# Three key tiles' halves kept in the second token group's buffer, with the hand-written order of steps rearranged

## The chip, the core and the metric

The kernel runs on one core of a Trainium2 chip. The metric is the device time of one execution in microseconds (us). Five engines take part: TensorE (PE, with its weight loads as PEld), VectorE (DVE), ScalarE (ACT), GpSimd (POOL) and SyncE (SP), which here only issues DMAs. Each engine works through its own queue in order. Tensors lie in on-chip memory in tiles of 128 partitions; PSUM holds the results of products.

## The reference

Local attention of 4 batches, 8 heads, 768 tokens, head size 64, and behind it a gated feed-forward layer over 3072 tokens (512 wide, 1536 inside):

```python
k_sum = k.reshape(B, H, nb, 32, D).max(axis=3)          # 24 block summaries
v_sum = v.reshape(B, H, nb, 32, D).mean(axis=3)
scores_l = scale * q @ k.T, masked to |i - j| < 16
scores_s = scale * q @ k_sum.T + log(32)
a = softmax(concat(scores_l, scores_s))
x = a @ concat(v, v_sum)                                # heads side by side: 512 wide
xn = x / sqrt(mean(x * x) + 1e-6) * rms_g
out = (silu(xn @ w_gate) * (xn @ w_val)) @ w_out
```

## The kernel before, in words

Tokens go in 24 units of 128 (six to a batch) and the feed-forward in token groups of 384, 128, 256 and then 384 tokens (`GROUPS`). Units 0 to 2 take a warm-up path of their own (`su_...` steps, float32). From unit 3 on a unit runs `load_unit`, `prep_q`, `prep_k`, `fill_k`, `prep_v`, `scores` and `expo` (twice, four heads each), `attend`, `norm_a` and `norm_b`. A group then runs, for each of twelve blocks f of 128 inner columns, `gate_val` (24 products into two PSUM tiles, then tanh and two multiplications) and `project` (the product with the output weights, added up in PSUM).

Precision is kept by splitting: a number is scaled by a power of two and held as a half-precision part and the half-precision rest. Weights are decoded and split on the way in (`decode_gv`, `split_gv`, `decode_o`); twelve gate and value blocks n, of which a pair (n even and odd) serves two f. `pow2` (L282) makes the powers of two in the small tiles `w_t`, `w_s`, `w_i`; `w_t` has one buffer.

The steps that the change touches:

- `split_k` (L468) makes the halves of a key tile in `khl`: ScalarE casts (L470), VectorE subtracts (L471), and SP transposes the result by DMA into `kT` (L476). `khl` has one buffer of 128 x 1024 half-precision numbers. `prep_k` (L493) calls it for tiles of 128 keys, `split_ks` (L465) for the block summaries (32 rows, into `ksT`).
- `fill_k` (L538) copies beside a key tile's own columns the summaries (from `ksT`), the last columns of the tile before (VectorE) and the first of the tile behind (GpSimd). `scores` (L561) of a unit needs the fills.
- `norm_b` (L803) transposes a normalised unit into its group's `xT`. The pool `xp` has two such buffers of 6144 half-precision numbers a partition, taken in turn by the groups.
- `sum_load` (L400) loads a piece of keys or values into `hn` (two buffers) and `sum_fold` (L412) reduces it, keys on VectorE and values on GpSimd.

`PLAN` (L43) is the list of steps. It gives the order in which instructions are written down, and thereby their priority: the build places each instruction on its engine's queue by a simulation of its own, when what it needs is ready there. So an engine's order follows `PLAN` without being the same.

Of the kernel before, what the change touches and what calls it, by code (L numbers as in the profile page):

```python
# [77 lines left out]
project 1 10 128 384; swap_att 3; gate_val 2 0 256; prep_k 9; gate_val 2 1 256; norm_a 6; project 2 0 256 512;  # L78
scores 7 1; gate_val 2 2 256; sum_load 2 0 0 2; fill_k 8; project 1 11 128 384; project 2 1 256 512;
sum_fold 2 0 0 0; load_k 10; scores 8 0; sum_fold 2 0 0 1; load_unit 9; sum_fold 2 0 0 2; gate_val 2 3 256; expo 7 1;  # L80
project 2 2 256 512; expo 8 0; sum_load 2 0 0 3; prep_q 9; project 0 11 384 0; prep_k 10; sum_fold 2 0 0 3;
gate_val 2 4 256; prep_k 11; scores 8 1; sum_load 2 0 1 0; prep_v 7; sum_load 2 0 1 1; expo 8 1; gate_val 2 5 256;
# [817 lines left out]
```

## Time and profile before

| | us |
|---|---|
| median of 3 runs (788.92 to 789.74) | 789.23 |
| the profiled execution | 787.48 |
| its span, first to last instruction | 785.7 |

| engine | busy us | share of the span |
|---|---|---|
| PE | 697.0 | 89% |
| DVE | 519.9 | 66% |
| ACT | 444.8 | 57% |
| POOL | 243.0 | 31% |

The span is the time from the first to the last instruction; the rest of an execution lies around it. An idle time of an engine is put down to what ended it (the releaser). An instruction waits for its engine's earlier ones as well as for its own inputs, so a releaser can be late because it stood behind another wait.

### The profile page before, as it was taken

Reading aid. Unit: us, or ns where it says so; the run is one execution under the profiler, and the core shown is the slowest. Engines: PE = TensorE matmul, PEld = TensorE weight load, DVE = VectorE, ACT = ScalarE, POOL = GpSimd, SP = SyncE. Lnnn points to the kernel's source line nnn. Section 1 sums busy time; section 2 is a strip of 40 time slices with the busy share of each in tenths; the row PEclk is TensorE's granted clock in tenths of the full one; section 3 lists DMA queues with packets and bytes.
Section 4 is the critical chain, followed back from the end, with each engine's and each line's share of the span. In section 5 each row is a group of like instructions: output and inputs, shape, how many; then the busy total and the mean of one; then the engine's idle time right before and its main releaser. Section 6 shows DMA issues by size and latency. Waiting matters only on the chain.

```text
span 785.7 us, 13988 instructions
## 1 busy us (share of the span) xinstructions
PE 697.0 (89%) x4880; PEld 488.5 (62%) x4880; DVE 519.9 (66%) x1466; ACT 444.8 (57%) x918; POOL 243.0 (31%) x334
## 2 busy tenths in 40 slices
PE   3871796629889999999999999999999999999997
PEld 2571454427667786666666665666666666666665
DVE  5799686967687686856767676677666664543222
ACT  3699857967556575744656565656455453421111
POOL 7355101554232244432223253422232221200000
PEclk9775798859999999999999999999999999999999
DMA  9944976578857947756756856775457452201001
GB/s 230 331 151 138 257 160 171 130 159 168 162 114 147 183 110 169 165 109 123 125 122 140 149 128 159 135 145 99 110 108 120 85 122 44 38 15 41 1 1 40
DMA packets 270547, 100.21 MB, mean 128 GB/s; under 512 B 254212, under 2 KB 254308, under 8 KB 270476
## 3 DMA queue, kind: packets, MB, share of 16 engines
q1 hardware_dynamic: 260700, 80.61, 50.7%
q10 hardware_dynamic: 7968, 16.78, 6.4%
q0 software_dynamic: 1808, 1.93, 1.1%
q8 instruction: 38, 0.62, 0.4%
q14 instruction: 33, 0.27, 0.1%
HBM read 51.38 MB, written 6.64 MB: 74 GB/s over the span
## 4 chain that ended last, share of the span: by engine, by line
PE 60%; DMA 15%; DVE 9%; issue 4%; SPq 4%; ACT 4%; POOL 4%; DVEq 0%; POOLq 0%; ACTq 0%
PE gv L829 36%; PE acc L854 18%; DMA kT<-khl 4%; PE att L614 3%; DMA hn<-in_k_dram 2%; DMA hn<-in_v_dram 2%; PE att L573 2%; SPq L484 2%; DMA qT<-qs 1%; DMA kr_l<-in_k_dram 1%; DVE khl L471 1%; POOL ee L226 1%; DMA eT<-ee 1%; PE acc L688 1%; DMA v1f<-in_v_dram 1%
## 5 line engine op out<-in xcount | busy, mean ns | idle before, releaser
L829 PE MATMUL gv<-xT,w_gv 128*128 128x384 f16 (+2 forms) x2592 | 408.8, 314 | 41.5 <-DMA xT<-xs 26.9
L829 PEld LDWEIGHTS <-w_gv 128*128 128x128 f16 x2592 | 241.4, 100 | 183.7 <-issue 56.4
L854 PE MATMUL acc<-wo,hh 128*128 128x512 f32 x576 | 188.9, 415 | 5.8 <-ACT hh L221 4.4
L226 POOL TENSOR_TENSOR ee<-sm,ee 128x512 f16<-128x512 f32 x84 | 84.1, 1020 | 151.1 <-ACT ee L221 117.1
L854 PEld LDWEIGHTS acc<-wo,hh 128*128 128x128 f32 x576 | 104.6, 190 | 26.5 <-ACT hh L221 5.0
L834 DVE SCALAR_TENSOR_TENSOR th<-th,gv 128x384 f32<-128x384 f32 (+2 forms) x108 | 54.5, 505 | 94.3 <-ACT th L833 94.0
L854 PE MATMUL acc<-wo,hl 128*128 128x512 f32 x288 | 111.1, 402 | 3.1 <-DVE hl L226 2.9
L588 ACT ACTIVATE sm<-sm,mx,c 128x192 f32<-128x192 f32 x168 | 78.4, 536 | 57.7 <-DVE mx L580 57.7
L833 ACT ACTIVATE th<-gv,f_sc 128x384 f32<-128x384 f32 (+2 forms) x108 | 57.8, 535 | 72.7 <-PE gv L829 68.1
L221 ACT CAST hh<-th 128x384 fp32r<-128x384 f32 (+2 forms) x108 | 51.0, 473 | 77.5 <-DVE th L835 76.6
L226 DVE TENSOR_TENSOR hl<-th,hh 128x384 fp32r<-128x384 f32 (+2 forms) x108 | 66.9, 619 | 40.3 <-ACT hh L221 39.9
L835 DVE SCALAR_TENSOR_TENSOR th<-th,f_sc,gv 128x384 f32<-128x384 f32 (+2 forms) x108 | 61.2, 567 | 27.6 <-PE gv L829 24.1
L854 PEld LDWEIGHTS acc<-wo,hl 128*128 128x128 f32 x288 | 53.7, 189 | 17.2 <-DVE hl L226 6.0
L577 DVE CUSTOM_DVE_ANT_0 sm<-att,mask 128x192 f32<-128x192 f32 x168 | 51.0, 350 | 11.3 <-POOL ee L226 9.7
L555 POOL DMA_DIRECT2D v2h<-v2h x42 | 22.9, 545 | 95.3 <-ACT v2h L554 95.3
L573 PE MATMUL att<-kT,qT 128*128 128x192 f16 x336 | 38.7, 253 | 10.3 <-DMA qT<-qs 9.9
L419 ACT ACTIVATE junk<-hn 96x512 uint8<-96x512 f32 x48 | 30.0, 626 | 24.2 <-DMA hn<-in_v_dram 14.3
L226 POOL TENSOR_TENSOR xs<-x,xs 128x512 f16<-128x512 f32 x24 | 31.6, 1317 | 34.5 <-ACT xs L221 32.5
L573 PEld LDWEIGHTS <-qT 128*128 128x128 f16 x336 | 27.1, 100 | 21.7 <-DMA qT<-qs 12.0
L221 ACT CAST ee<-sm 128x512 f16<-128x512 f32 x84 | 38.5, 506 | 3.7 <-DMA eT<-ee 3.5
L614 PEld LDWEIGHTS <-eT 128*128 128x128 f16 x840 | 30.8, 99 | 8.8 <-issue 6.6
L425 POOL TENSOR_TENSOR hn<-hn 96x512 f32<-96x512 f32 x18 | 25.3, 1408 | 24.9 <-DMA hn<-in_v_dram 22.3
(162 smaller groups left out, 876.6 us busy)
## 6 DMA issues: line engine op xcount, KB each, us to landing
out_dram<-ob ACTq DMA_DIRECT2D x23, 256.0 KB
hn<-in_k_dram SPq DMA_DIRECT2D x24, 192.0 KB
hn<-in_v_dram SPq DMA_DIRECT2D x24, 192.0 KB
qr_l<-in_q_dram SPq DMA_DIRECT2D x17, 256.0 KB
vr_l<-in_v_dram SPq DMA_DIRECT2D x17, 256.0 KB
raw<-in_moe_w_val_dram ACTq DMA_DIRECT2D x4, 1024.0 KB
kr_l<-in_k_dram SPq DMA_DIRECT2D x16, 256.0 KB
raw<-in_moe_w_gate_dram ACTq DMA_DIRECT2D x3, 1024.0 KB
```

The lines of the kernel that those rows point to most:

```text
L221: nc.scalar.copy(o, i)
L226: (nc.vector if ENG.get(op, "p") == "v" else nc.gpsimd).tensor_tensor(o, a, b, op=ALU.subtract)
L419: nc.scalar.activation(junk[0:96], y[:, o:o + DM], AF.Square, accum_out=d["ss"][:, j:j + 1])
L573: nc.tensor.matmul(pt[:, j * SC:(j + 1) * SC], lhsT=s["qT"][:, a * H + h, :], rhs=kT[:, h, :], start=(a == 0), stop=(a == 1))
L577: nc.vector.tensor_tensor_reduce(sm[:, i, :], pt[:, j * SC:(j + 1) * SC], mask, 1.0, NEG, op0=ALU.add, op1=ALU.max, accum_out=mx[:, i:i + 1])
L588: nc.scalar.activation(sm[:, i, :], sm[:, i, :], AF.Exp, scale=s["c"][:, 0:1], bias=mx[:, i:i + 1])
L614: nc.tensor.matmul(po[r][:, h // 2, 0:D + 1], lhsT=e, rhs=vv[:, 0:D + 1], start=(n == 0), stop=(n == len(pairs) - 1))
L829: nc.tensor.matmul(pt[:, 0:T], lhsT=w_gv[:, f - f % 2 + i, wi, c, f % 2, :], rhs=x[:, xi, c, 0:T], start=(n == 0), stop=(n == 3 * NC - 1))
L833: nc.scalar.activation(th[:, 0:T], pg[:, 0:T], AF.Tanh, scale=f_sc[:, f - f % 2:f - f % 2 + 1])
L834: nc.vector.scalar_tensor_tensor(th[:, 0:T], th[:, 0:T], 1.0, pg[:, 0:T], op0=ALU.add, op1=ALU.mult)
L835: nc.vector.scalar_tensor_tensor(th[:, 0:T], th[:, 0:T], f_sc[:, f - f % 2 + 1:f - f % 2 + 2], pv[:, 0:T], op0=ALU.mult, op1=ALU.mult)
L854: nc.tensor.matmul(accs[grp][j], lhsT=h[:, js], rhs=wo_hl[f // 2][:, wi, f % 2, :], start=(f == 0 and n == 0), stop=(f == NF - 1 and n == 2))
```

## The change

`split_k` takes its buffer for the first three tiles of 128 keys (in PLAN's order the key tiles 3, 2 and 4) from a new list `spare`: three rooms of 1024 numbers a partition in one `xT` buffer that is taken before any group's. The first group's `xT` then takes the other buffer, and the second group's the one with the rooms. All later calls, and the summaries', take `khl` as before. The tile `w_t` gets a second buffer. PLAN lists the same steps with the same arguments in another order. The differing lines of PLAN run from its first to `load_k 18` in the fifth of the groups of 384; the excerpt keeps those from the end of the warm-up to the beginning of group 2.

```diff
 PLAN = """
-su_first; su_load 1 1; su_load 0 1; su_load 0 0; su_load 4 1; su_q 0; su_load 3 1; su_k 3; load_gv 1 1; su_load 2 1;
...
-su_expo 1 0; split_gv 1; su_attend 1 0; load_gv 3 1; load_gv 4 1; su_attend 1 1; su_scores 2 0; norm_a 0;
-su_expo 2 0; su_attend 2 0; su_scores 2 1; decode_gv 3; split_gv 2; load_o 2 1; su_square 0 5; su_expo 2 1;
-load_o 0 1; su_attend 2 1; norm_a 1; norm_b 0; su_square 1 0; norm_a 2; split_gv 3; su_square 1 2; decode_o 0;
-decode_gv 4; su_square 0 0; norm_b 1; su_square 1 5; su_square 1 3; split_gv 4; decode_o 2; su_square 1 1;
-sum_load 1 0 0 0; sum_load 1 0 0 2; sum_fold 1 0 0 0; gate_val 0 2 384; sum_fold 1 0 0 1; prep_k 4; decode_gv 5;
-split_gv 5; decode_o 4; prep_k 5; prep_q 3; decode_gv 6; load_gv 7; fill_k 3; sum_load 1 0 0 3; load_o 8;
-sum_fold 1 0 0 2; sum_load 1 0 1 1; sum_load 1 0 1 0; prep_v 3; load_o 6; decode_gv 7; project 0 0 384 0; fill_k 5;
-scores 3 0; expo 3 0; load_gv 8; sum_fold 1 0 0 3; sum_load 1 0 1 2; split_gv 6; sum_fold 1 0 1 0; sum_load 1 0 1 3;
-project 0 1 384 0; load_gv 9; load_o 10; scores 3 1; split_gv 7; sum_fold 1 0 1 1; sum_fold 1 0 1 2; decode_o 6;
-sum_scale 1 0; sum_fold 1 1 0 0; project 0 2 384 0; prep_q 4; decode_gv 8; split_gv 8; sum_load 1 1 0 2;
-sum_load 1 1 0 3; sum_load 1 1 1 0; sum_fold 1 1 0 1; project 0 3 384 0; fill_k 4; project 0 4 384 0;
-split_ks 1; sum_fold 1 1 0 3; sum_fold 1 1 1 0; decode_gv 9; load_unit 5; project 0 5 384 0; split_gv 9; scores 4 0;
-sum_load 1 1 1 2; decode_gv 10; load_gv 11; sum_fold 1 1 1 1; expo 4 0; prep_q 5; load_k 6; sum_fold 1 1 1 2;
-norm_b 3; gate_val 0 6 384; scores 4 1; gate_val 0 7 384; gate_val 1 0 128; decode_o 10; sum_load 1 1 1 3;
-sum_fold 1 1 1 3; swap_att 2; decode_gv 11; load_unit 6; load_k 7; prep_k 6; gate_val 1 1 128; project 1 0 128 384;
-split_gv 10; prep_v 4; gate_val 0 8 384; gate_val 0 9 384; project 0 6 384 0; project 1 1 128 384; gate_val 1 2 128;
-expo 4 1; project 0 7 384 0; gate_val 1 3 128; split_gv 11; prep_q 6; scores 5 0; prep_k 7; attend 4;
-project 1 2 128 384; project 1 3 128 384; swap_right; gate_val 1 4 128; norm_a 4; fill_k 6; scores 5 1;
-project 0 8 384 0; scores 6 0; load_k 8; scores 6 1; sum_load 2 0 0 1; sum_scale 1 1; gate_val 1 5 128;
-gate_val 0 10 384; expo 5 0; expo 5 1; project 1 4 128 384; gate_val 1 6 128; project 1 5 128 384; load_unit 7;
-project 1 6 128 384; expo 6 0; prep_q 7; norm_b 4; gate_val 1 7 128; prep_v 5; gate_val 0 11 384; expo 6 1; attend 5;
-prep_k 8; gate_val 1 8 128; load_k 11; norm_a 5; project 0 9 384 0; norm_b 5; project 1 7 128 384;
-project 0 10 384 0; gate_val 1 9 128; gate_val 1 10 128; fill_k 7; scores 7 0; expo 7 0; load_unit 8; load_k 9;
-gate_val 1 11 128; prep_v 6; attend 6; project 1 8 128 384; prep_q 8; project 1 9 128 384; sum_load 2 0 0 0;
...
+su_first; su_load 0 1; load_gain; su_load 1 1; su_load 0 0; su_load 4 1; su_q 0; su_load 3 1; su_k 3; load_gv 1 1;
...
+load_gv 5; su_expo 1 0; split_gv 1; su_attend 1 0; load_gv 4 1; su_scores 2 0; su_square 0 5; norm_a 0;
+su_attend 1 1; su_expo 2 0; su_attend 2 0; su_scores 2 1; decode_gv 3; split_gv 2; load_o 2 1; su_expo 2 1;
+load_o 0 1; su_attend 2 1; norm_a 1; norm_b 0; su_square 1 0; norm_a 2; decode_o 0; su_square 1 2; decode_gv 4;
+su_square 0 0; split_gv 3; norm_b 1; su_square 1 5; su_square 1 3; split_gv 4; decode_o 2; su_square 1 1;
+sum_load 1 0 0 0; sum_load 1 0 0 2; sum_fold 1 0 0 0; sum_fold 1 0 0 1; decode_gv 5; split_gv 5; decode_o 4;
+prep_k 4; prep_k 5; prep_q 3; fill_k 5; sum_fold 1 0 0 2; decode_gv 6; load_gv 7; fill_k 3; sum_load 1 0 0 3;
+load_o 8; scores 3 0; load_o 6; sum_load 1 0 1 1; decode_gv 7; expo 3 0; sum_load 1 0 1 0; prep_v 3; load_gv 8;
+sum_fold 1 0 0 3; sum_load 1 0 1 2; split_gv 6; project 0 0 384 0; load_o 10; sum_fold 1 0 1 0; scores 3 1;
+sum_load 1 0 1 3; project 0 1 384 0; sum_fold 1 0 1 1; gate_val 0 2 384; sum_fold 1 0 1 2; decode_o 6; load_gv 9;
+sum_fold 1 1 0 0; decode_gv 8; split_gv 7; project 0 2 384 0; sum_scale 1 0; prep_q 4; sum_load 1 1 0 2;
+sum_load 1 1 0 3; split_gv 8; sum_load 1 1 1 0; sum_fold 1 1 0 1; project 0 3 384 0; project 0 4 384 0;
+split_ks 1; sum_fold 1 1 0 3; decode_gv 9; load_unit 5; fill_k 4; load_gv 11; project 0 5 384 0; sum_fold 1 1 1 0;
+split_gv 9; scores 4 0; sum_load 1 1 1 2; decode_gv 10; gate_val 0 6 384; load_k 6; project 0 6 384 0; norm_b 3;
+sum_load 1 1 1 3; sum_fold 1 1 1 1; split_gv 10; sum_fold 1 1 1 2; gate_val 0 7 384; expo 4 0; prep_q 5;
+gate_val 1 0 128; scores 4 1; sum_load 2 0 0 1; decode_o 10; prep_k 6; sum_fold 1 1 1 3; swap_att 2;
+project 1 0 128 384; decode_gv 11; load_unit 6; load_k 7; gate_val 1 1 128; prep_v 4; gate_val 0 8 384;
+gate_val 0 9 384; sum_load 2 0 0 0; gate_val 1 2 128; project 1 1 128 384; expo 4 1; project 0 7 384 0;
+gate_val 1 3 128; split_gv 11; scores 5 0; prep_k 7; attend 4; project 1 2 128 384; swap_right; prep_q 6; fill_k 6;
+scores 5 1; project 0 8 384 0; scores 6 0; gate_val 1 4 128; expo 5 0; norm_a 4; load_k 8; scores 6 1;
+project 1 3 128 384; sum_scale 1 1; gate_val 1 5 128; gate_val 0 10 384; expo 5 1; project 1 4 128 384;
+project 1 5 128 384; load_unit 7; gate_val 1 6 128; project 1 6 128 384; expo 6 0; prep_q 7; norm_b 4;
+gate_val 1 7 128; prep_v 5; gate_val 0 11 384; attend 5; expo 6 1; prep_k 8; norm_a 5; project 0 9 384 0;
+gate_val 1 8 128; project 1 7 128 384; load_k 11; project 0 10 384 0; gate_val 1 9 128; gate_val 1 10 128; fill_k 7;
+norm_b 5; scores 7 0; expo 7 0; load_unit 8; project 1 8 128 384; prep_q 8; load_k 9; gate_val 1 11 128; prep_v 6;
...
@@ -281,7 +281,7 @@
 
         def pow2(ss, n, name, floor, shift=0):
             bufs = 1 if name == "g" else 2
-            t = sp.tile([P, n], I32, name=f"{name}_t", bufs=1)
+            t = sp.tile([P, n], I32, name=f"{name}_t", bufs=1 + (name == "w"))
             s = sp.tile([P, n], I32, name=f"{name}_s", bufs=bufs)
             i = sp.tile([P, n], I32, name=f"{name}_i", bufs=bufs)
             nc.vector.tensor_scalar(t, ss.bitcast(I32), 24, None, op0=ALU.logical_shift_right)
@@ -465,8 +465,12 @@
         def split_ks(b):
             sums[b]["kst"] = split_k(sums[b]["ksr"], sums[b]["sk"], 32)
 
+
+        spare = xp.tile([P, 2, NC, 384], F16, name="xT").rearrange("p a c t -> p (a c t)")
+        spare = [spare[:, 2 * DM * i:2 * DM * (i + 1)].rearrange("p (h d) -> p h d", h=H) for i in range(3)]
+
         def split_k(src, s, n):
-            hl = ap.tile([n, H, P], F16, name="khl")
+            hl = spare.pop(0) if n == P and spare else ap.tile([n, H, P], F16, name="khl")
             nc.scalar.activation(hl[:, :, 0:D], src, AF.Copy, scale=s[0:n])
             nc.vector.scalar_tensor_tensor(hl[:, :, D:P], src, s[0:n], hl[:, :, 0:D], op0=ALU.mult, op1=ALU.subtract)
             if n == P:
```

## Rows read from the trace of the kernel before

**Rows 1.** The page's engines: busy us, share of the span, instructions.

```profile
PE 697.0 (89%) x4880; PEld 488.5 (62%) x4880; DVE 519.9 (66%) x1466; ACT 444.8 (57%) x918; POOL 243.0 (31%) x334
```

**Rows 2.** Stages: length, busy us (instructions) per engine, clock, DMA share, GB/s.

```profile
83.00:129.00 46.00, 43.27 (x238) 27.97 (x239) 33.40 (x83) 32.39 (x58) 4.51 (x10) 0.94 0.84 206
129.00:136.00 7.00, 1.34 (x6) 0.43 (x5) 4.53 (x13) 4.99 (x8) 2.62 (x7) 0.77 0.39 85
136.00:151.50 15.50, 13.85 (x98) 8.89 (x96) 14.75 (x37) 13.71 (x27) 8.50 (x8) 0.88 0.49 125
151.50:173.00 21.50, 2.87 (x19) 2.52 (x19) 17.00 (x33) 17.08 (x33) 11.41 (x11) 0.62 0.70 148
...
181.00:320.00 139.00, 127.97 (x1166) 98.79 (x1163) 102.83 (x331) 84.84 (x202) 50.66 (x61) 0.98 0.76 151
320.00:786.00 466.00, 457.62 (x3097) 310.75 (x3094) 276.78 (x797) 223.48 (x481) 115.76 (x142) 0.99 0.47 96
```

**Rows 3.** TensorE in order of time: start, us, operation, [idle before, its releaser].

```profile
83.06 6.67 PE L829 MATMUL gv<-xT,w_gv 128*128 128x384 f16 x24 [17.55 <-DMA xT<-xs]
89.56 0.51 PE L442 MATMUL att<-kv_ss,ones 128*128 128x6 f32 x4
...
118.76 0.82 PE L573 MATMUL att<-kT,qT 128*128 128x192 f16 x8
...
131.42 0.50 PE L829 MATMUL gv<-xT,w_gv 128*128 128x384 f16 x2 [1.78 <-ACT w_gv L385]
135.79 5.60 PE L829 MATMUL gv<-xT,w_gv 128*128 128x384 f16 x22 [3.87 <-DVE w_gv L386]
...
160.75 2.74 PE L573 MATMUL att<-kT,qT 128*128 128x192 f16 x16 [9.23 <-DMA qT<-qs]
172.89 2.72 PE L829 MATMUL gv<-xT,w_gv 128*128 128x128 f16 x24 [9.39 <-DMA xT<-xs]
```

**Rows 4.** The chain of waits: start, us, what.

```profile
99.88 7.74 DMA kT<-khl
...
114.48 3.47 DMA kT<-khl
...
119.57 9.15 DMA kT<-khl
```

**Rows 5.** ScalarE in order of time, casts of key halves.

```profile
92.13 0.70 ACT L470 ACTIVATE khl<-wo,kv_s 128x512 f16<-128x512 f32 x1
...
107.65 0.72 ACT L470 ACTIVATE khl<-kr,kv_s 32x512 f16<-32x512 f32 x1 [4.41 <-DMA kT<-khl]
```

**Rows 6.** VectorE in order of time.

```profile
107.65 0.21 DVE L223 COPY kT<-kT 128x192 f16<-128x192 f16 x1 [2.83 <-DMA kT<-khl]
...
110.04 0.28 DVE L223 COPY qs<-qs 128x512 f16<-128x512 f16 x1
...
131.47 0.36 DVE L577 CUSTOM_DVE_ANT_0 sm<-att,mask 128x192 f32<-128x192 f32 x1 [4.55 <-POOL ee L226]
...
158.85 1.27 DVE L386 SCALAR_TENSOR_TENSOR w_gv<-w,w_s,w_gv 128x1024 f16<-128x1024 f32 x1
```

**Rows 7.** GpSimd in order of time.

```profile
128.77 0.52 POOL L223 COPY kT<-kT 128x128 f16<-128x128 f16 x2 [7.03 <-DMA kT<-khl]
```

**Rows 8.** SP's queue in order of time.

```profile
111.45 1.91 SPq L535 DMA_TRANSPOSE qT<-qs  x1
```

**Rows 9.** ScalarE in order of time, towards the end of the warm-up.

```profile
73.55 1.13 ACT L328 ACTIVATE w<-wo 128x1024 f32<-128x1024 f32 x1
...
75.63 0.60 ACT L221 CAST xs<-x 128x512 f16<-128x512 f32 x1
```

**Rows 10.** SP's waits, 83 to 185 us: us in total, times, longest.

```profile
SPq L409 <- DVE hn L425: 10.5, 4, 5.4
```

**Rows 11.** Loads of 1 MB issued from ScalarE's queue.

```profile
99.89 0.37 ACTq L360 DMA_DIRECT2D wo<-in_moe_w_out_dram  x1
...
119.57 0.38 ACTq L360 DMA_DIRECT2D wo<-in_moe_w_out_dram  x1
```

More of the change, by code (lines that the diff above doesn't have):

```diff
@@ L78 @@
[L78 to L82, printed above, removed]
@@ L88 @@
-sum_load 2 1 0 1; project 2 9 256 512; scores 9 1; gate_val 3 1 384; sum_scale 2 0; split_ks 2; load_unit 11;
-project 2 10 256 512; sum_fold 2 1 0 1; project 2 11 256 512; project 3 0 384 768; sum_load 2 1 0 2;
-sum_fold 2 1 0 2; expo 9 1; sum_load 2 1 0 3; sum_load 2 1 1 1; scores 10 0; project 3 1 384 768; prep_v 9; attend 9;
-sum_load 2 1 1 0; gate_val 3 2 384; norm_a 9; scores 10 1; gate_val 3 3 384; gate_val 3 4 384; load_k 14;
-sum_fold 2 1 0 3; fill_k 11; prep_q 11; sum_fold 2 1 1 0; sum_fold 2 1 1 1; norm_b 9; expo 10 0; project 3 2 384 768;
@@ L93 @@
-gate_val 3 5 384; sum_load 2 1 1 2; gate_val 3 6 384; load_k 12; project 3 3 384 768; prep_v 10; expo 10 1;
-sum_load 2 1 1 3; scores 11 0; sum_fold 2 1 1 2; project 3 4 384 768; project 3 5 384 768; attend 10; scores 11 1;
-sum_fold 2 1 1 3; expo 11 0; gate_val 3 7 384; project 3 6 384 768; project 3 7 384 768; norm_a 10; prep_k 12;
-expo 11 1; load_unit 12; norm_b 10; gate_val 3 8 384; sum_scale 2 1; load_k 13; prep_q 12; gate_val 3 9 384;
-project 3 8 384 768; prep_k 13; prep_v 11; sum_load 3 0 0 0; attend 11; gate_val 3 10 384; prep_k 14; load_unit 13;
@@ L98 @@
-norm_a 11; gate_val 3 11 384; norm_b 11; load_k 15; fill_k 12; gate_val 4 0 384; prep_q 13; gate_val 4 1 384;
-project 3 9 384 768; scores 12 0; expo 12 0; fill_k 13; scores 12 1; gate_val 4 2 384; expo 12 1;
-project 4 0 384 1152; sum_fold 3 0 0 0; scores 13 0; scores 13 1; sum_load 3 0 0 1; gate_val 4 3 384; expo 13 0;
-prep_v 12; project 4 1 384 1152; project 4 2 384 1152; prep_k 15; attend 12; gate_val 4 4 384; load_unit 14;
-fill_k 14; prep_q 14; expo 13 1; prep_v 13; norm_a 12; sum_load 3 0 0 2; sum_fold 3 0 0 1; project 4 3 384 1152;
@@ L108 @@
-fill_k 15; load_k 17; project 4 8 384 1152; load_unit 16; attend 14; prep_v 15; prep_q 16; sum_fold 3 0 1 3;
-scores 15 0; gate_val 4 10 384; sum_load 3 1 0 0; norm_a 14; expo 15 0; norm_b 14; prep_k 17; project 4 9 384 1152;
-sum_scale 3 0; sum_fold 3 1 0 0; sum_load 3 1 0 1; load_ks 3; gate_val 4 11 384; sum_fold 3 1 0 1;
-project 4 10 384 1152; scores 15 1; gate_val 5 0 384; sum_load 3 1 0 2; split_ks 3; fill_k 16; sum_fold 3 1 0 2;
-sum_load 3 1 0 3; expo 15 1; project 4 11 384 1152; scores 16 0; gate_val 5 1 384; sum_fold 3 1 0 3;
@@ new lines @@
+sum_fold 2 0 0 1; expo 7 1; project 2 2 256 512; expo 8 0; sum_load 2 0 0 3; prep_q 9; sum_fold 2 0 0 2;
+project 0 11 384 0; gate_val 2 4 256; scores 8 1; prep_k 11; prep_k 10; sum_fold 2 0 0 3; sum_load 2 0 1 0; prep_v 7;
+sum_load 2 0 1 1; expo 8 1; gate_val 2 5 256; norm_b 6; gate_val 2 6 256; attend 7; norm_a 7; sum_fold 2 0 1 0;
+norm_b 7; prep_v 8; project 2 3 256 512; attend 8; project 2 4 256 512; sum_load 2 0 1 2; fill_k 9; fill_k 10;
+sum_fold 2 0 1 1; load_unit 10; project 2 5 256 512; project 2 6 256 512; norm_a 8; gate_val 2 7 256; scores 9 0;
@@ new lines @@
+project 3 7 384 768; norm_a 10; expo 11 1; load_unit 12; norm_b 10; sum_scale 2 1; load_k 13; gate_val 3 8 384;
+prep_q 12; gate_val 3 9 384; project 3 8 384 768; prep_k 13; prep_v 11; sum_load 3 0 0 0; attend 11;
+gate_val 3 10 384; prep_k 14; gate_val 3 11 384; load_unit 13; norm_a 11; norm_b 11; fill_k 12; load_k 15;
+gate_val 4 0 384; prep_q 13; gate_val 4 1 384; project 3 9 384 768; scores 12 0; expo 12 0; fill_k 13; scores 12 1;
+gate_val 4 2 384; sum_fold 3 0 0 0; scores 13 0; scores 13 1; expo 12 1; sum_load 3 0 0 1; gate_val 4 3 384;
@@ new lines @@
+load_k 16; sum_fold 3 0 1 0; expo 14 0; norm_b 13; sum_load 3 0 1 1; prep_k 16; project 4 6 384 1152; expo 14 1;
+gate_val 4 8 384; sum_fold 3 0 1 1; sum_load 3 0 1 2; project 4 7 384 1152; gate_val 4 9 384; sum_fold 3 0 1 2;
+sum_load 3 0 1 3; fill_k 15; load_k 17; project 4 8 384 1152; load_unit 16; attend 14; prep_v 15; prep_q 16;
+sum_fold 3 0 1 3; scores 15 0; gate_val 4 10 384; sum_load 3 1 0 0; norm_a 14; expo 15 0; norm_b 14; prep_k 17;
+project 4 9 384 1152; sum_scale 3 0; sum_fold 3 1 0 0; sum_load 3 1 0 1; load_ks 3; gate_val 4 11 384;
@@ L118 @@
+sum_load 3 1 1 3; gate_val 5 4 384; fill_k 17; sum_fold 3 1 1 3; project 5 3 384 1536; scores 17 0; gate_val 5 5 384;
+load_k 18; sum_scale 3 1; expo 17 0; project 5 4 384 1536; attend 16; load_k 19; load_unit 18; prep_v 17; norm_a 16;
 gate_val 5 6 384; prep_q 18; prep_k 18; norm_b 16; project 5 5 384 1536; prep_k 19; gate_val 5 7 384; scores 17 1;
```

48 lines of the change are left out of this document (28 added, 20 removed).

## The prediction

> **What bounds the kernel now.** I read the views in this order: the page's list of engines, a table of stages, TensorE's instructions in order of time, then the queues that its waits point at. TensorE is busy for 89% of the span [rows 1]. From 320 us on it works 457.6 of 466 us, from 181 to 320 us 128.0 of 139 [rows 2]: behind the warm-up the kernel has almost nothing left but products, so time won earlier should reach the end nearly whole, and only there is time to be won. From 83 to 129 us TensorE is full too, with the gate and value products of the first token group. [...]
>
> Where the chain comes from is seen in the chain of waits. Between 99.88 and 128.72 us three transposes of key halves stand in it with 7.74, 3.47 and 9.15 us, 20.4 us together [rows 4]. They are in series because `split_k` (L468) has a single buffer `khl`: ScalarE may write the next halves only when the transpose of the last has read them. ScalarE's casts show it: the first at 92.13, the 32-row one only at 107.65, after 4.41 us idle until a transpose had landed [rows 5]. ScalarE, VectorE and GpSimd run in order, so the wait spreads: VectorE stood 2.83 us before a fill at 107.65, with the second swap of unit 3's queries (110.04) behind it [rows 6]; GpSimd stood 7.03 us before two fills at 128.77, and the halves of unit 3's first exponentials (`ee`) were queued behind them [rows 7]. VectorE waited 4.55 us for those at 131.47 [rows 6], and TensorE's 3.87 us for `w_gv` at 135.79 [rows 3] came out of that. The first local scores, at 118.76, could run only when the fourth key tile had landed at 117.95 [rows 3, 4].
>
> **Part 1: three rooms.** Nothing is added: the same casts, subtractions and transposes, with other addresses. The buffer stands free until the second group's `xT` is written, some 50 us later. What goes is the order among tiles 3, 2, 4 and the 32-row sums, in which four transposes in series become three without a mutual wait and one alone in `khl`. Before: from the first cast at 92.13 to 117.95, 25.8 us [rows 4, 5]. After: three casts of 0.72 us and subtractions beside them put the last transpose on its queue at about 97 us if they run together; PLAN now puts tile 4 behind two decodes, so I don't count on that. The binding one is the 32-row cast: ScalarE was free for it at 103.24 (107.65 less 4.41), and it needs 0.72 [rows 5], VectorE's subtraction as much, and a landing between 3.47 and 7.74 us [rows 4], hence 108.5 to 113 with some hand-over. The queries of unit 3, issued at 111.45 [rows 8], lose the 2.83 us and the 32-row halves that stood ahead, and land by 110 to 114. So unit 3's scores start at 110 to 114 and not at 118.76: 5 to 9 us, I take 7, the middle, since both landings are in this range already.
>
> Tile 5 still shares `khl` with the sums. Its cast can follow their landing at 108.5 to 113, and it lands 1.5 + 3.47 to 1.5 + 9.15 us later with an issue between, 114 to 124 instead of 128.72: 5 to 14 us sooner, 9 taken. Then GpSimd's 7.03 us before the fills is gone or short, and the exponentials wait for their own cast, 7 us sooner. What is late next is the same sequence behind it, moved: unit 3's second scores, its attention, `norm_b 3`, the `xT` of group 1.
>
> **What reaches TensorE.** At 131 to 136 us it gets back 1.78 + 3.87 = 5.65 us. Its next work, 13.9 us from 136 to 151.5 [rows 2], then ends 5.65 us sooner, and the two releasers of the 18.6 us behind it come 7 to 9 us sooner. So TensorE leaves the hole 5.65 to 9 us sooner; I take 8, nearer to the releasers, because the hole ends with them. It is taken off whole, as 24.3 us of idle cover it, and TensorE's later work follows. The lower clock there (0.62 to 0.88 [rows 2]) stays as it is: 0, bounds 0 to 2 us gained.
>
> **Part 2: a second `w_t`.** VectorE's next weight shift need no longer wait for GpSimd's read of the last. Cover: VectorE idles in the hole anyway. 0, bounds 0 to 1.2 us gained (one GpSimd step queued late).
>
> **Part 3: the order.** PLAN is a priority, not the order on the engines: `sum_scale` stands before `gate_val 0 0` in PLAN and ran behind it, at 89.56 [rows 3]. So a moved step moves only where two are ready together. The front: `norm_a`, `decode_o 0`, `decode_gv 4` and `split_gv 3` change places around the three norms that lead to 83.06, where TensorE had waited 17.55 us [rows 3]. The last normalised tile was cast at 75.63 [rows 9] without idle time before it; one decode of two passes like the 1.13 us one before it [rows 9] costs 2.3 us, one less gives as much, and twice that is the most I see moved: 0, bounds -4.6 to +4.6. `gate_val 0 2` goes behind `project 0 1`: TensorE has nothing else ready at that point, so 0, bound +4 us (one such pair of products). The second half of weight 9 was finished at 160.1 [rows 6], yet the products of `gate_val 0 8` stand behind `gate_val 1 0` in TensorE's queue, which waited until 172.89; in the new PLAN that remains, so 0, bound -9.4. Of two loads for batch 2, `sum_load 2 0 0 1` goes up past `prep_k 6`, `load_unit 6` and `load_k 7` on SP's queue and `sum_load 2 0 0 0` past `prep_k 7` and `prep_q 6`, transposes and loads. They wait for a free `hn`, and everything on SP waits with them. Four such waits cost 10.5 us between 83 and 185 us, the longest 5.4 [rows 10]. Value 0, bound +10.8 for two of the longest.
>
> **Sum.** 787.5 us of the profiled execution (785.7 of span and 1.8 around it) less 8 is 779.5. The median of the runs shown is 1.75 above that execution, and so is my number: 789.2 - 8 = 781.2.
>
> **The rivals.**
> (a) The new order takes part of the other idle too, by filling the wait before 172.89 with `gate_val 0 8` (two of its halves, 3.9 us each) or by a front that is 4.6 us shorter: 789.2 - 12 to 789.2 - 16, and 769 with 7.8 and 4.6 both. For it: the work was ready at 160.1. Against it: PLAN's sequence there is as before.
> (b) Nothing is won, 789: the transposes issued sooner land as late. Beside the load of an output weight issued at 99.89 a transpose took 7.74 us, beside the next one at 119.57 another took 9.15, between them one took 3.47 [rows 4, 11]. Three at once, from 94 us, meet the same loads (the DMA engines were 84% busy from 83 to 129 us [rows 2]). Against it: the serial waits on ScalarE and VectorE go even so. [...]
> (c) Slower: the two raised loads hold SP. They decide once their waits exceed the 8 us won and 1.6 us more. Two of the longest, 5.4 us each, with a hand-over to the attention of unit 4 or 5 and none of it hidden: 781 + 10.8 = 792. For it: `hn` has two buffers, and the folds of v, which free them, are GpSimd's, the engine with the wait of 7 us [rows 7]. Against it: the order on SP is by readiness too, as on TensorE.
>
> [...]
>
> **How the numbers follow.** Forecast 781 (776 to 786): 0.50. (a) 769 to 776: 0.13. (b) 787.7 to 790.8: 0.15. (c) 791 to 798, 792 its centre: 0.22. About 0.2%, 1.6 us, can be told from no change. Faster than 787.6: 0.50 + 0.13 = 0.63. Same: (b) without the 0.01 of it that may lie above 790.8, 0.14. Slower: 0.22 and that 0.01. The range that leaves out a fifth reaches from 769, the far end of (a), to 793, past the centre of (c).
>
> **What would show it.** Right: three casts of key halves on ScalarE without idle time for a transpose between them, first local scores at 110 to 114 us, the fills on GpSimd without a 7 us wait, no wait for `w_gv` of 4 us, the second group's first product at about 165 us instead of 172.89, and the idle time before it still there in size. Wrong: key transposes that land near 118 us all the same (b); waits of SP for `hn` ahead of `qT` or `eT` transposes between 150 and 200 us (c); a first product far from 83 us, which would be the order's doing and not the rooms'.

## The result and the profile after

The change made the kernel slower, not faster: 793.23 us (median of 8 runs, 789.63 to 796.05) against 789.49 for the kernel before in the same set, ratio 1.006 with a 95% interval of 1.0038 to 1.0082. Measured once more later, the same program gave 1.0026 (1.0005 to 1.0048); what is known of the difference is told below. The forecast was 781.2. The profiled execution of after spans 792.2 us, that of before 785.7.

The stages of after, with the columns of [rows 2] (length, busy us and instructions of PE, PEld, DVE, ACT, POOL, clock, DMA share, GB/s):

```profile
83.00:129.00 46.00, 42.25 (x231) 26.75 (x231) 32.60 (x82) 32.65 (x58) 4.26 (x12) 0.93 0.79 204
129.00:136.00 7.00, 3.53 (x16) 2.16 (x17) 5.91 (x15) 6.73 (x13) 2.13 (x5) 1.00 0.45 111
136.00:151.50 15.50, 11.58 (x90) 8.43 (x89) 11.36 (x33) 12.80 (x23) 5.80 (x5) 0.86 0.50 125
151.50:173.00 21.50, 4.58 (x16) 2.83 (x16) 16.48 (x21) 11.33 (x19) 14.85 (x13) 0.50 0.38 89
...
320.00:786.00 466.00, 461.14 (x3149) 314.18 (x3147) 277.99 (x803) 227.04 (x489) 119.69 (x149) 1.00 0.48 96
```

The hole, TensorE's idle time from 129 to 173 us (before, the four waits of [rows 3] there add up to 24.3 us), is still there, and the granted clock in its long part is now 0.50 instead of 0.62. TensorE of after in order of time, as in [rows 3]:

```profile
83.47 6.89 PE L833 MATMUL gv<-xT,w_gv 128*128 128x384 f16 x24 [17.51 <-DMA xT<-xs]
119.96 0.82 PE L577 MATMUL att<-kT,qT 128*128 128x192 f16 x8
...
135.31 3.75 PE L833 MATMUL gv<-xT,w_gv 128*128 128x384 f16 x22 [2.86 <-DVE w_gv L386]
148.27 0.24 PE L618 MATMUL att<-v1h,eT 128*128 128x65 f16 x1 [3.89 <-DMA eT<-ee]
...
169.69 1.46 PE L577 MATMUL att<-kT,qT 128*128 128x192 f16 x8 [13.98 <-DMA qT<-qs]
175.24 1.44 PE L577 MATMUL att<-kT,qT 128*128 128x192 f16 x8 [3.82 <-DVE mx L581]
177.28 2.72 PE L833 MATMUL gv<-xT,w_gv 128*128 128x128 f16 x24 [0.61 <-DMA xT<-xs]
```

The first product after the warm-up comes at 83.47 (before 83.06), so the reordered front won and lost nothing. Unit 3's first scores come at 119.96, not sooner than the 118.76 of before. In this execution the scores of unit 4 come at 169.69 instead of 160.75, and the second group's first product at 177.28 instead of 172.89, 4.4 us later. In the other profiled execution of the same program (`after_again`, span 784.9 us) that product came at 170.59, 2.3 us sooner than before: between the two, 6.7 us at this product became 7.3 us of span. So the loss that the rows of this section show is one that not every execution has.

The rooms themselves do what the change says. ScalarE of after (start, us, line, what), and behind it SP's queue:

```profile
91.94 1.94 ACT L474 ACTIVATE xT<-wo,kv_s 128x512 f16<-128x512 f32 x3
93.79 0.71 ACT L474 ACTIVATE khl<-kr,kv_s 32x512 f16<-32x512 f32 x1
```
```profile
157.72 0.32 SPq L409 DMA_DIRECT2D hn<-in_v_dram  x1
...
164.46 0.33 SPq L409 DMA_DIRECT2D hn<-in_v_dram  x1
...
165.35 2.82 SPq L539 DMA_TRANSPOSE qT<-qs  x1
```

Three casts and the 32-row one run back to back from 91.94 (before, the 32-row cast ran at 107.65 after a wait of 4.41 us [rows 5]). The rows of SP show a part of the loss: two loads of `hn` (`sum_load 1 1 0 2` and `1 1 0 3`) stand ahead of unit 4's queries, each held until a fold frees a buffer, and the transpose `qT` goes out at 165.35. Before, it was issued at 155.32, with the second of these loads behind it:

```profile
155.32 3.45 SPq L535 DMA_TRANSPOSE qT<-qs  x1
158.94 0.47 SPq L409 DMA_DIRECT2D hn<-in_v_dram  x1
```

The load explains only a part of these 10.0 us. The last copy that makes the queries ready, on VectorE, before and in after:

```profile
154.11 0.28 DVE L223 COPY qs<-qs 128x512 f16<-128x512 f16 x1
```
```profile
160.69 0.27 DVE L223 COPY qs<-qs 128x512 f16<-128x512 f16 x1
```

The queries were ready at 154.39 before and at 160.96 in after, 6.6 us later, since VectorE's new order has them behind unit 3's attention results and value splits. SP then held them for 4.4 us instead of 0.9. In PLAN `prep_q 4` stands ahead of both loads before and after; it is the build that placed the transpose behind the second.

The second group's first product waits for something else besides: unit 3's norm. Its step `x_r` on GpSimd stands behind the fold of that second load, before and in after:

```profile
162.50 1.26 POOL L425 TENSOR_TENSOR hn<-hn 96x512 f32<-96x512 f32 x1 [3.54 <-DMA hn<-in_v_dram]
...
165.39 0.57 POOL L800 TENSOR_TENSOR x_r<-x_r,consts 128x1 f32<-128x1 f32 x1
```
```profile
167.71 1.26 POOL L425 TENSOR_TENSOR hn<-hn 96x512 f32<-96x512 f32 x1 [3.28 <-DMA hn<-in_v_dram]
168.93 0.57 POOL L804 TENSOR_TENSOR x_r<-x_r,consts 128x1 f32<-128x1 f32 x1
```

From the issue of this load to that product pass 13.9 us before (158.94 to 172.89) and 12.8 in after (164.46 to 177.28), and 12.3 to 13.9 in all seven traces in which the norm has this place. One of them is `after_q4` below, where the queries went out 17 us sooner and the product came at 173.63 all the same. So in these traces the product follows that load and its fold, and not the queries.

### The profile page after: what moved, and what is told of

Read it like the earlier page. It is cut to its first block, busy times and chain, and to the rows that moved or that the text cites. A ratio compares the mean times of both kernels' runs of the same rounds, so it can differ in the third digit from the quotient of the medians.

```text
span 792.2 us, 13970 instructions
## 1 busy us (share of the span) xinstructions
PE 698.4 (88%) x4880; PEld 488.6 (62%) x4880; DVE 522.6 (66%) x1466; ACT 445.1 (56%) x918; POOL 245.1 (31%) x334
## 4 chain that ended last, share of the span: by engine, by line
PE 55%; DVE 13%; DMA 12%; ACT 8%; issue 5%; SPq 4%; POOL 3%; DVEq 0%; ACTq 0%; POOLq 0%
PE gv L833 32%; PE acc L858 17%; DMA hn<-in_k_dram 4%; SPq L488 2%; PE att L618 2%; PE att L577 2%; ACT sm L592 2%; DVE hl L226 1%; DMA eT<-ee 1%; DMA hn<-in_v_dram 1%; DVE sm L581 1%; DMA qT<-qs 1%; PE acc L692 1%; DMA v1f<-in_v_dram 1%; DVE th L839 1%
## 5 line engine op out<-in xcount | busy, mean ns | idle before, releaser
L833 PE MATMUL gv<-xT,w_gv 128*128 128x384 f16 (+2 forms) x2592 | 403.2, 312 | 33.4 <-DMA xT<-xs 18.1
L226 DVE TENSOR_TENSOR hl<-th,hh 128x384 fp32r<-128x384 f32 (+2 forms) x108 | 71.3, 660 | 39.5 <-ACT hh L221 37.4
L425 POOL TENSOR_TENSOR hn<-hn 96x512 f32<-96x512 f32 x18 | 28.3, 1572 | 30.9 <-DMA hn<-in_v_dram 26.7
```

The lines of the kernel that those rows point to most:

```text
L226: (nc.vector if ENG.get(op, "p") == "v" else nc.gpsimd).tensor_tensor(o, a, b, op=ALU.subtract)
L833: nc.tensor.matmul(pt[:, 0:T], lhsT=w_gv[:, f - f % 2 + i, wi, c, f % 2, :], rhs=x[:, xi, c, 0:T], start=(n == 0), stop=(n == 3 * NC - 1))
```

## The experiments

All compare with the kernel before on the same chip (788.41, 787.05, 787.31, 788.36 and 788.51 us in the five sets).

| kernel | us | ratio (95% interval) |
|---|---|---|
| `rooms_held` | 786.76 | 0.9986 (0.9966 to 1.0006) |
| `order_held` | 799.23 | 1.0147 (1.0112 to 1.0183) |
| `code_only` | 803.26 | 1.0193 (1.0162 to 1.0224) |
| `plan_only` | 800.50 | 1.016 (1.0131 to 1.0188) |
| `splits_free` | 789.00 | 1.001 (0.9989 to 1.0031) |
| `after_q4` | 791.25 | 1.0052 (1.0031 to 1.0073) |
| `after_q4n3` | 789.70 | 1.0037 (1.002 to 1.0053) |
| `rooms_q4n3` | 795.35 | 1.0105 (1.0081 to 1.0129) |
| `before_nl` | 789.61 | 1.0024 (1.0005 to 1.0044) |
| `rooms_nl` | 788.70 | 1.0023 (1.0004 to 1.0042) |
| `after_nl` | 786.87 | 0.9981 (0.996 to 1.0002) |
| `after_open` | 788.34 | 1.0014 (0.9991 to 1.0037) |
| `after_open3` | 790.90 | 1.0038 (1.001 to 1.0065) |
| `after_open4` | 793.55 | 1.0066 (1.0038 to 1.0094) |
| `after_one_wt` | 788.84 | 1.0019 (0.9993 to 1.0044) |
| `after_again` | 790.38 | 1.0026 (1.0005 to 1.0048) |
| `after_one_wt2` | 789.49 | 1.0022 (0.9998 to 1.0047) |
| `after_open_one_wt` | 788.89 | 1.0011 (0.9991 to 1.0031) |

### The rooms and the order, one without the other

Where an order is "held", each instruction of an engine is told to stand behind the one that preceded it in the named kernel, so that the build cannot rearrange the queues.

```diff
 rooms_held: PLAN of before, every queue held as in before
-            hl = ap.tile([n, H, P], F16, name="khl")
+            hl = spare.pop(0) if n == P and spare else ap.tile([n, H, P], F16, name="khl")
 code_only: the same code and PLAN, nothing held
 plan_only: code of before, PLAN of after, nothing held
 order_held: code of before, PLAN and queues of after (the fifteen instructions of the five key splits left free)
```

> The three rooms and the second w_t, with the PLAN of before and with every engine's instructions kept in exactly the order that they have in the kernel before. Only waits differ. Theory P (the prediction's: the waits for key transposes hold up TensorE, and the new order lost more than they gave): first local scores at 110 to 114 us instead of 118.8, 780 to 784 us against 789.5 before. Theory Q (the rooms' gain is hidden: with the keys early, the first local scores wait for unit 3's queries or for the next transfer, as they do in the changed kernel at 119.96): scores still at 117 to 119 us, 787 to 791 us.

> The new PLAN without the rooms and with one w_t; all instructions are kept in the order that they have on their engines in the changed kernel, but for the 15 of the five key splits (tiles 2 to 5 and the sums), which cannot stand there with a single buffer and are left to the build. Theory P: the order costs what the rooms give and 4 us more, 799 to 803 us. Theory Q: the rooms give the changed kernel next to nothing, so it comes out near it, 791 to 797 us.

> The rooms and the second w_t with the PLAN of before, engines' orders left to the build (which places instructions anew, as keys are ready sooner in its simulation). Theory P: 780 to 786 us. Theory Q: 787 to 792 us, and its distance from the run with the held order is the price of the build's own rearranging.

> The new PLAN without the rooms and with one w_t, engines' orders left to the build. Theory P: 795 to 803 us. Theory Q: the order is the whole cost, 791 to 797 us.

The rooms alone are within the noise, just under theory Q's range; their scores came at 120.04, later than either theory had them. The order alone costs 1.5%, as theory P had it, with the fifteen instructions left free as a reservation; with nothing held (`plan_only`) it costs 1.6%. `code_only` surprised both theories: with more buffers the build arranged the queues in another way, and that cost 1.9%. So a change of buffers can here bring a change of order with it. With the new PLAN the same code came to 793.23 and 790.38 instead of 803.26. Why the rooms alone win nothing is in the chain of waits of `rooms_held` (start, us, what), and in VectorE's queue:

```profile
99.59 7.65 DMA kT<-xT
114.10 3.46 DMA kT<-xT
119.00 9.29 DMA kT<-khl
```
```profile
107.27 0.21 DVE L223 COPY kT<-kT 128x192 f16<-128x192 f16 x1 [2.55 <-DMA kT<-xT]
...
108.99 0.73 DVE L475 SCALAR_TENSOR_TENSOR khl<-kr,kv_s,khl 32x512 f16<-32x512 f32 x1
```

The same three transposes, within 0.2 us as long as in [rows 4]; two now start from rooms that nobody waits for. The fill at 107.27 waits for the landed tile as data, 2.55 us against 2.83 [rows 6], and the subtraction of the 32 rows stands in the same queue behind it. So the single buffer was one reason for the series, and the order of the queue was another.

In the new order the rooms do count. Without them (`order_held`) ScalarE waits for transposes between its casts, and TensorE loses 7.5 us in a stage that was full (34.80 us busy of 46, against 42.25 in after):

```profile
103.86 0.72 ACT L470 ACTIVATE khl<-kr,kv_s 32x512 f16<-32x512 f32 x1 [1.64 <-DMA kT<-khl]
...
115.25 0.72 ACT L470 ACTIVATE khl<-wo,kv_s 128x512 f16<-128x512 f32 x1 [3.98 <-DMA kT<-khl]
```
```profile
83.00:129.00 46.00, 34.80 (x166) 20.90 (x167) 26.09 (x60) 24.89 (x42) 3.12 (x9) 0.84 0.70 174
```

### The key splits early and together, the rest as before

```diff
 splits_free: rooms_held, but prep_k 2 to 5 and split_ks 0 are not held
```

> Rooms and second scale buffer, every engine in the order of the kernel before except the fifteen instructions of the five key splits, which stand early and together (three casts, then three transposes, in a row). Theory R (the rooms are worth something once casts and transposes are moved together and the rest of the order is kept): first local scores of unit 3 at 112 to 116 us instead of 118.76, total 782 to 786. Theory S (something after the keys binds, the queries of unit 3 or the exchanged weights of expert 0): scores at 118 to 120, total 786 to 790.

Three casts ran together from 92.64 and no key transpose is left in the chain of waits. It won nothing, and unit 3's scores came later:

```profile
121.97 0.82 PE L577 MATMUL att<-kT,qT 128*128 128x192 f16 x8
```
```profile
107.08 0.69 DVE L425 TENSOR_TENSOR hn<-hn 96x512 f32<-96x512 f32 x1 [4.25 <-DMA hn<-in_k_dram]
107.69 0.60 DVE L839 SCALAR_TENSOR_TENSOR th<-th,f_sc,gv 128x384 f32<-128x384 f32 x1
```

Theory S comes nearest, with scores a little later than its 118 to 120. The row of the scores has no idle time before it: TensorE arrives there in its order, after products that it does without a gap from 108.35 on. There it had waited 3.34 us for a `th` that stood on VectorE behind a fold, and that fold had waited 4.25 us for its load.

### Unit 4's queries, and unit 3's norm, brought forward

```diff
 after_q4, SP:  load_ks 1
+               prep_q 4
                sum_load 1 1 0 2; load_unit 5 (five loads); sum_load 1 1 0 3; load_unit 5 (one load)
-               prep_q 4
 ScalarE: the cast of prep_q 4 ahead of those of prep_v 4; VectorE: its subtraction and copies ahead of attend 3
 after_q4n3 besides: norm_a 3 and norm_b 3 ahead of sum_fold 1 1 0 2 (ScalarE, GpSimd) and sum_load 1 1 0 3 (SP)
 rooms_q4n3: the same two moves in rooms_held
```

> The kernel after with unit 4's queries brought forward alone: cast ahead of the value casts, subtraction and copies ahead of unit 3's attention results, transpose on SyncE ahead of the load of the third sum chunk. Theory T (the new order costs its time through this one late transfer, landing at 169.7): scores of unit 4 at 155 to 160, total 782 to 786. Theory U (two chains end close together: the second half of unit 4's scores waits for VectorE behind unit 3's norm, and the product waits for the norm's transpose): first half of the scores early, first product of the second token group still at 175 to 178, total 791 to 793.

> The same, and unit 3's norm (square, scale on GpSimd, casts, transpose) brought ahead of the folds and loads of the sum chunks on all four queues. Theory T: as with the queries alone, 782 to 786. Theory U: first product of the second group at 164 to 170 instead of 177.28, total 781 to 786, and at least 6 us better than with the queries alone. If the folds that are pushed back bind next, the gain is under 4 us (789 or more).

> The rooms in the order of the kernel before (786.76 measured), with the same two chains brought forward. Theory U: first product at 164 to 168 instead of 172.7, total 778 to 782, faster than the kernel before by 0.8 to 1.3 per cent. Theory T (the order of before has no such late transfer): no gain, 785 to 788.

The queries alone came to 791.25 us, in theory U's range: the second half of the scores then waited 16.5 us for VectorE, and the first product came at 173.63, a little sooner than U's 175 to 178. Both moves bring it to 171.37. That missed theory U's 164 to 170 and its 781 to 786 us; what came is the last branch, that the folds pushed back bind next. Against the 1.0026 of after's second measurement, neither kernel (1.0052 and 1.0037) gains anything, and the execution of after with the span of 784.9 us had this product at 170.59. After `after_q4n3`'s first product the next wait follows:

```profile
171.37 2.77 PE L833 MATMUL gv<-xT,w_gv 128*128 128x128 f16 x24
177.29 7.17 PE L833 MATMUL gv<-xT,w_gv 128*128 128x128 f16 x48 [3.15 <-DVE th L838]
```

`rooms_q4n3` refutes my 778 to 782. The first product came at 167.40, 5 us earlier, and then TensorE stood:

```profile
183.40 0.99 PE L376 MATMUL att<-w_ss,ones 128*128 128x1 f32 x4 [13.28 <-ACT qs L534]
```
```profile
164.29 1.23 SPq L818 DMA_TRANSPOSE xT<-xs  x1
165.58 0.57 SPq L409 DMA_DIRECT2D hn<-in_v_dram  x1
```

The norm's transpose now held the load of `hn` behind it (158.94 in before, 165.58 here), the folds and unit 5's queries came later, and 1% was lost. It is the fault of the change with the places exchanged: here the norm's transpose was moved ahead of the load on SP's queue, and the load waited instead.

### The loads of the sums left out

The second batch's sums take their first quarter four times; twelve of sixteen loads are left out, all squares and folds stay. Each queue keeps its order.

```diff
             w = 4 * DM // NPC
+            if b == 1 and z:
+                return
             y = ap.tile([96, w], F32, name="hn", bufs=2)
...
-            y = d.pop(("y", h2, z))
+            y = d["x"] if b == 1 and z else d.pop(("y", h2, z))
```

> The kernel before, every engine in its order, but twelve of the sixteen loads of the second batch's sums are left out (its sums take their first quarter four times; squares and folds stay). Theory V (these loads hold SyncE, and with it the queries and norms behind them, so they set when the second token group opens): first product of the second group at 160 to 167 us instead of 172.9, total 778 to 784. Theory W (another chain sets the opening): 171 to 174, total 786 to 789.

> The rooms and the second scale buffer in the order of the kernel before, with the same twelve loads left out. If the prediction's 8 us of the rooms were only covered by the loads of the sums: scores of unit 3 at 108 to 113 us, and the total 4 to 8 us under that of the kernel before with the loads left out. If the fills and the weights of expert 0 bind as well: within 2 us of it.

> The kernel after, every engine in its order, with the same twelve loads left out. Theory V (the new order costs what it costs by standing one more of these loads ahead of unit 4's queries and by a later fold): the total comes within 2 us of the kernel before with the loads left out, or under it, instead of 5.6 us over. Theory W (the order costs elsewhere): still 4 to 7 us over it.

This turns the sign. Without these loads the new order is not slower than the old one but faster: 0.9981 (0.996 to 1.0002) against 1.0024 (1.0005 to 1.0044), two intervals that do not meet. So the loss of the change goes with these loads, as theory V had it for the new order. The runs take out twelve loads at once, though, and move other waits with them (the old order became 0.2% slower); no run moves the one load `sum_load 1 1 0 3` alone. In the old order, theory V is refuted: the opening stays where it was. There the fold ahead of unit 3's norm now waits for a square on ScalarE and starts at 163.58; in `after_nl` it starts at 159.12. The first products of the second group, in `before_nl` and `after_nl`:

```profile
173.40 2.72 PE L831 MATMUL gv<-xT,w_gv 128*128 128x128 f16 x24 [8.56 <-DMA xT<-xs]
```
```profile
168.50 2.72 PE L835 MATMUL gv<-xT,w_gv 128*128 128x128 f16 x24 [0.20 <-DMA xT<-xs]
```

The rooms bring nothing to the old order here either (`rooms_nl` 1.0023).

### One hold after another taken away

```diff
 after_open: after_q4n3, and
+VectorE: scores 4 0 (row maxima) right behind split_ks 1; gate_val 1 0 and 1 1 ahead of what waits for unit 6's keys
+ScalarE: expo 4 0 (exponentials) and gate_val 1 0 ahead of sum_fold 1 1 0 3
 after_open3 besides: scores 4 1, the rest of expo 4 0, gate_val 1 1 and 0 8 ahead of prep_k 6
 after_open4 besides: prep_q 5 ahead of prep_k 6 and 7
```

> The kernel after with queries of unit 4 and norm of unit 3 brought forward (789.7 measured) and, besides, unit 4's first row maxima ahead of the weight decoding on VectorE and the first two gate steps of the second group ahead of the folds and casts that wait for loads. If each hold is worth what the wait behind it shows: first product at 163 to 167 us, no 3 us wait for the gate behind it, total 781 to 786, under both kernels. If the next hold takes it over: 787 to 790.

> The kernel after with the opening of the second group brought forward as before (788.34 measured) and the next hold taken away too: unit 4's second row maxima, its exchanged weights and the first gate steps stand ahead of the key work of unit 6 on VectorE, ScalarE and GpSimd, and the weights' transpose ahead of the next key load on SyncE. If the 8.7 us wait at 181 us was the whole remainder: that wait goes, total 780 to 784. If the queries of unit 5 and the gates behind it hold the same span: the wait moves to 176 to 195 us and the total stays at 786 to 789.

> The same, and unit 5's queries as well ahead of the key work of units 6 and 7. If holds in a row are the whole cause: 778 to 783, under both kernels. If TensorE then runs into work that needs the sums of the second batch, whatever the order: 785 to 789.

In `after_open` the first product comes at 161.10, 11.8 us earlier than before and 16.2 earlier than in after's first execution (163.55 and 161.41 in the other two). The gain is given back behind it. The longest of the waits that follow, in `after_open`, `after_open3` and `after_open4`:

```profile
161.10 2.72 PE L833 MATMUL gv<-xT,w_gv 128*128 128x128 f16 x24 [0.52 <-DMA xT<-xs]
...
181.22 1.19 PE L858 MATMUL acc<-wo,hh 128*128 128x512 f32 x2 [8.67 <-DVE kT L223]
```
```profile
197.60 1.44 PE L833 MATMUL gv<-xT,w_gv 128*128 128x128 f16 x12 [9.84 <-DVE q_t L287]
```
```profile
194.52 1.44 PE L833 MATMUL gv<-xT,w_gv 128*128 128x128 f16 x12 [11.60 <-DVE th L838]
```

None of these versions beats the kernel before. `after_open` fell where the next hold takes over; `after_open3` and `after_open4` (790.90 and 793.55) came out above both of their ranges. That the waits are holds of queue order and no need for the sums was my guess; it is not shown, since each move also pushed the key work of units 6 and 7 back.

### One scale buffer, and the same program twice

```diff
-            t = sp.tile([P, n], I32, name=f"{name}_t", bufs=1 + (name == "w"))
+            t = sp.tile([P, n], I32, name=f"{name}_t", bufs=1)
 after_one_wt, after_one_wt2: one program, the queues of after; after_again: after itself
 after_open_one_wt: after_open with one buffer
```

> The kernel after, every engine in its order, with one scale buffer for the weights instead of two. The prediction put the second buffer at 0 to 1.2 us: 793 to 794.5. If the early scales of the second token group use the second buffer in the new order: 796 or more.

> The kernel after once more, the same program, beside the next kernel on the same chip. If the second scale buffer costs what the first look at one buffer said: 4 to 5 us over the next kernel (792 to 794.5). If that look differed by the chip or by chance: within 1.5 us of it (789 to 792).

> One scale buffer in the order of after, the same program as the first look, once more. If its gain is real: 787.5 to 790. If it was chance: 791 to 794. In its trace GpSimd's second exchange of weights takes under 3 us (5.2 us in the kernel after) if the gain comes from which engine is ahead when VectorE and GpSimd run side by side.

> The opening of the second group brought forward (788.34 with two scale buffers) with one scale buffer. If both gains are real and stand in different waits: 783 to 786, under both kernels. If they win the same wait: 787 to 789.

The first measurement of one buffer (788.84, under both of its ranges) promised 4 us; side by side the two differ by 0.9 us, within the noise (`after_one_wt2` by itself lies in the range for a real gain), and `after_open_one_wt` with 788.89 is no faster than `after_open`. No price of the second buffer can be told from the noise, and what looked like one is spread between executions of one program: `after_again` ran from 786.65 to 796.34 us over 12 runs, the kernel before, in that set, from 785.45 to 790.35 over 29. The two profiled executions of after span 792.2 and 784.9 us, with the same instructions in the same order. They part on GpSimd. First the execution of 792.2 us, then that of 784.9:

```profile
151.30 2.76 POOL L292 TENSOR_SCALAR w_i<-w_t 128x1 int32<-128x1 int32 x1 [6.86 <-DVE w_t L287]
...
155.42 2.27 POOL L425 TENSOR_TENSOR hn<-hn 96x512 f32<-96x512 f32 x1
...
161.14 3.29 POOL L425 TENSOR_TENSOR hn<-hn 96x512 f32<-96x512 f32 x1 [3.12 <-DMA hn<-in_v_dram]
```
```profile
148.39 1.16 POOL L292 TENSOR_SCALAR w_i<-w_t 128x1 int32<-128x1 int32 x1 [6.89 <-DVE w_t L287]
...
151.18 1.29 POOL L425 TENSOR_TENSOR hn<-hn 96x512 f32<-96x512 f32 x1
...
155.32 1.87 POOL L425 TENSOR_TENSOR hn<-hn 96x512 f32<-96x512 f32 x1 [1.84 <-DMA hn<-in_v_dram]
```

Up to the attention product at 148.27 and 145.36 they are 2.9 us apart; at the transpose of unit 4's queries (165.35 and 158.11) 7.2. Of the 4.3 us between, 4.0 are one scale of 128 numbers that took 2.4 times as long (2.76 against 1.16) and two folds that took 1.8 times as long, and each late fold held the load of `hn`, and with it SP: the loads went out 0.03 us behind the ends of the folds, at 157.72 and 164.46 against 152.50 and 157.22. Two more executions have the same order of the queues: in `after_one_wt2` (span 787.8) the scale is long too, and the ready queries were held on SP for 4.4 us, as in the execution of 792.2; in `after_one_wt` (785.5), as in that of 784.9, the scale is short and the hold 0.2 us. So in these four executions the loss comes with the long scale and folds, and the two without them span what the kernel before does (785.7). The expectation that a short weight exchange on GpSimd would go with the faster time failed: it took 2.78 us in `after_one_wt2` and 5.22 in the faster execution of after.

## Why the prediction was wrong

**The bound, and the chain read as its cause.** That TensorE is full except in the hole holds. That time won there reaches the end nearly whole holds only in part: between two executions of one order 6.7 us of it did, but where the time was won by moving work, it was lost again behind the hole (`after_open` opens the second group 11.8 us sooner than the kernel before and is no faster; `rooms_q4n3` opens it 5 us sooner and is 1% slower). The step that failed first is "The first local scores, at 118.76, could run only when the fourth key tile had landed at 117.95". The row of 118.76 [rows 3] has no wait in brackets: TensorE was working until that moment, 43.27 us of 46 in the stage [rows 2]. TensorE's only waits in the 18 us ahead of it are these:

```profile
108.38 0.96 PE L854 MATMUL acc<-wo,hl 128*128 128x512 f32 x3 [0.37 <-DVE hl L226]
110.83 4.06 PE L829 MATMUL gv<-xT,w_gv 128*128 128x384 f16 x24 [1.49 <-DVE th L834]
```

So behind the products that stand ahead of them in TensorE's queue, the scores could have come 1.9 us sooner at most, and what the keys cost through VectorE, whose fill at 107.65 waits for a key transpose [rows 6], is in these 1.9 us. The chain of waits led through GpSimd's fills to unit 3's weights; it was a chain of releases and not a chain of lost time of TensorE. "Unit 3's scores start at 110 to 114" did not come true in any version: 119.96 in after, 120.04 in `rooms_held`, 121.97 in `splits_free`. An order of TensorE with the scores ahead of some of those products was not tried.

**Part 1, "in series because `split_k` has a single buffer".** Half right. ScalarE's 4.41 us wait went, as said; the series stayed in the old order, because fills that need the landed tiles stand in VectorE's and GpSimd's queues. The 8 us were 0 (`rooms_held` 0.9986, `rooms_nl` equal to `before_nl`). Of the 5.65 us of waits for `w_gv`, 1.6 went in `rooms_held` (0.42 and 3.64 remain) and 2.4 in after (0.35 and 2.86), so the larger part did not come out of the keys. In the new order the rooms are worth 0.9 to 1.2% (`order_held` 1.0147 against 1.006 and 1.0026), as far as its fifteen free instructions allow the comparison; no step of the sum had that.

**Part 2, the second `w_t`: 0.** Right, within 0.9 us.

**Part 3, the order: 0 with a bound of +10.8.** Here the sign was decided. Held alone the order costs 1.5%. The front (bounds of 4.6 us both ways) moved 0.4 us. The loads of batch 2 that I named did not hold anything that mattered; SP waited 1.4 us ahead of the first and not at all ahead of the second. Another load of the same kind did, the fourth of batch 1's values, `sum_load 1 1 0 3`. In the execution of 792.2 us it went out 5.5 us later than before (164.46 against 158.94), held ready queries for 4.4 us, and its fold came 5.2 us later (167.71 against 162.50), with unit 3's norm behind it, and the second group's first product 4.4 us later. What the prediction lacked is the path from this load over its fold to the norm, and the spread of the folds' own times: in the four executions of this order the loss came with the long ones.

**The rivals.** (c) had the mechanism (a load of `hn` that holds SP ahead of `qT`) with the wrong load. Its time, 792, is near the first median by luck: it is 781 with the 8 us of the rooms won, which were not, and 10.8 us of waits for two loads that cost 1.4. (b), that transposes issued sooner land as late, failed as stated: in `splits_free` all left the chain. Nothing was won even so. (a) did not occur; the first of its times, 789.2 - 12 = 777.2, also lies above the 769 to 776 that it is given. The range to 793 missed the first median by 0.2 us and held the second, 790.38. "What would show it" named the right places: the first product far from 165 and SP waiting for `hn` ahead of `qT`.

**What stays open.** How much of the 0.3 to 0.6% is the place of the load and how much the longer folds on GpSimd; the runs without the loads take both away, and none moves this load alone. Why the folds are long in some executions only is not shown.

## What to carry to other kernels

Before a chain of waits is priced, find out whether the engine that sets the end waits at its steps at all: a transfer that lands just before its reader is no loss if the reader was busy (here the landing at 117.95 and the scores at 118.76, with no idle time before them). In queues that run in order, as here, a buffer removes a wait only if nothing else in the queue needs the same landing (the fill in `rooms_held` still waited 2.55 us of 2.83), and a step moved ahead of a waiting load exchanges the two waits (in `rooms_q4n3` the load went out at 165.58 instead of 158.94); follow what was won to the end before it is counted. Hold the order of all queues before a change of buffers is judged; here the build's rearranging alone moved the time by 2%.

## What the runs showed of the hardware

A GpSimd instruction on 128 numbers, mostly 0.19 us elsewhere (the median of the twelve in after), took 1.16 and 2.76 us in two executions of one program, and a fold 1.29 and 2.27. Beside the shorter one VectorE ran in the main one instruction (`L386`, 1.27 us), beside the longer one three instructions in a row:

```profile
151.12 1.27 DVE L386 SCALAR_TENSOR_TENSOR w_gv<-w,w_s,w_gv 128x1024 f16<-128x1024 f32 x1
152.32 1.22 DVE L342 SCALAR_TENSOR_TENSOR w<-raw,w 128x1024 uint32<-128x1024 uint32 x1
153.45 0.55 DVE L226 TENSOR_TENSOR hl<-th,hh 128x384 fp32r<-128x384 f32 x1
```

The scale ends at 151.30 + 2.76 = 154.06 us, 0.06 after the last of these (154.00); in the other execution at 149.55, 0.06 after VectorE's `L386` (148.22 + 1.27). That such neighbours on VectorE make the whole spread of 786.65 to 796.34 us is my guess; no run shows it.
